# Two thirds of the probability tiles transposed by DMA instead of TensorE, in a top-k attention and MLP-mixer kernel

## The chip, the cores and the metric

The kernel runs on one core of one Trainium2 chip. The metric is the device time of one execution in microseconds (us); the median of several runs is given. Five engines work side by side, each through its own instructions in order: TensorE (PE in the profile; its weight loads are PEld), VectorE (DVE), ScalarE (ACT), GpSimd (POOL) and SyncE (SP), which here only issues DMAs.

## The reference

Attention over 8 batches and 8 heads, 576 rows of 64 channels; each row of scores keeps its 32 largest entries. The heads are then laid side by side as 512 channels, and an MLP-mixer follows: a token MLP (576 to 256 to 576), added to its input, and a channel MLP (512 to 1536 to 512), added again.

```python
scores = scale * np.matmul(q, k.transpose(0, 1, 3, 2))
kth = np.partition(scores, -top_k, axis=-1)[..., -top_k:-top_k + 1]
mask = scores >= kth
scores = np.where(mask, scores, -1000000000.0)
scores = scores - np.max(scores, axis=-1, keepdims=True)
attn = np.exp(scores)
attn = attn / (np.sum(attn, axis=-1, keepdims=True) + 1e-09)
return np.matmul(attn, v).astype(np.float32)
...
xt = x.transpose(0, 2, 1)
h = np.maximum(xt @ w_tok1, 0.0) @ w_tok2
u = x + h.transpose(0, 2, 1)
h2 = np.maximum(u @ w_ch1, 0.0) @ w_ch2
return (u + h2).astype(np.float32)
```

## The kernel before

**Units.** The work is cut into 32 units, one for each pair of heads of a batch. A unit's scores are nine tiles of 128 rows by 576 columns: tiles 0 to 7 are rows t*128 on of head 0 or 1 (t, hh = divmod(i, 2)), tile 8 holds the last 64 rows of both heads. Group 0 is tiles 0 to 3, group 1 is tiles 4 to 8. After every fourth unit a batch is complete and its channel MLP follows.

**A unit, step by step.** SP loads q, k and v two units ahead (load_one). PE transposes q and k (qk_tr), ACT copies them out. PE computes the scores in fp32 (s0_mm, s1_mm, st_mm), and ACT copies them from PSUM to the tiles SS and St. VectorE finds each row's 32nd largest score. It takes the maximum of the two halves of each row (upper, L350, writes hi), pairs the quarters of that (split4, L374, hh and hl), and takes four rounds of eight maxima from hh, with match_replace between them (top_round, L385 and L388). GpSimd meanwhile finds the minimum of each pair by integer arithmetic: both_bits (L356) adds the two halves' bits, lower_bits (L365) subtracts the maximum's bits. VectorE takes eight maxima each from hl and from these minima (low_round, L398), and combine (L406 to L419) merges the lists into the threshold kthall.

**Mask and transpose.** ACT takes the exponential of each whole tile (expo, L456, writes E in bf16), with minus the row's maximum as bias (neg_max, L447, on GpSimd, behind the first round). A second tile U is zero where the score reaches the threshold and positive below it. Tiles 1, 3, 5, 7 and 8 get U in one ACT instruction (below_act, L492), the other four in two on GpSimd (below, L469, through z, and clamp, L477). PE multiplies E by the identity and U by the identity times -2^100, both into one PSUM tile tpp: transposed, and far below zero wherever the entry is masked. There are four blocks of 128 columns, two matmuls each (p_tr, L498 and L501); the last 64 columns of several tiles go together into tpl (ptail_tr). ACT evicts both through a Relu into PT, the transposed probabilities (p_ev, L521 and L525; ptail_ev, L541 and L549). PE multiplies PT by v and a column of ones (o_mm, L562), VectorE takes the reciprocal of the sums (rden, L574), and ACT scales O into Xb (o_ev). The token MLP of the unit's 128 channels follows, on PE and ACT.

**The order of work.** No order is written by hand. Each step is a task with an engine, an estimated duration, a priority (lower goes first; U is 100 times the unit), the tasks it depends on, and the buffers it takes and gives back. The class Plan plays all tasks through once at build time; the times at which they start there give the order of instructions of each engine. A result reaches another engine LAG = 0.25 us late in the plan, plus a slack given to the task. At run time only data and buffers are waited for, but each engine keeps its order: a late result holds up whatever stands behind the instruction that waits. The reciprocal rden has the slack RSLACK:

```python
r = add("DVE", 0.3, U - 500, lambda hh=hh: o_den(st, hh), deps=[om], acq=[("den", u, hh)],
        slack=0.0 if last else RSLACK)
```

GpSimd's masks of a group stand behind lower_bits of the next group (the lists hold and later), and both_bits of a group depends on neg_max, and so on the first round. The last unit's group 1 takes its masks on VectorE (below_dve, L485).

Of the kernel before, what the change touches and what calls it, by code (L numbers as in the profile page):

```python
# [10 lines left out]
BIG = 3.0e38  # L11
LAG = 0.25
RSLACK = 3.0
ACTMASK = (1, 3, 5, 7, 8)
PE_RATE = 0.85


# [88 lines left out]
def kernel(  # L106
# [23 lines left out]
    P = 128  # L130
# [28 lines left out]
    qktp = pool("qktp", 2)  # L159
    ssp = pool("ssp", 4)  # L160
    stp = pool("stp", 2)
    gp = pool("gp", 2)
    eep = pool("eep", 9)
    uup = pool("uup", 8)
    m8p = pool("m8p", 3)
    mgp = pool("mgp", 1)
# [36 lines left out]
    lbufs = [const.tile([P, NS, 2, NLO], f32, name=f"lb{i}", tag=f"lb{i}") for i in range(2)]  # L203
    for t in lbufs:
        nc.gpsimd.memset(t[:, :, :, 0:1], BIG)
    kthall = const.tile([P, NU * NTILE], f32, tag="kthall")
    low8 = const.tile([P, NU * NTILE, 2], f32, tag="low8")
    lists = {
        key: const.tile([P, NS, w], f32, name=key, tag=key)
        for key, w in (("hi", HALF), ("lo", HALF), ("hh", QUAR), ("hl", QUAR))  # L210
    }
    ctr = {"vb": 0, "lb": 0}

    def take(kind, bufs):
        x = bufs[ctr[kind] % len(bufs)]
# [121 lines left out]
    def srow(st, i):  # L337
        return st["St"][:, :] if i == 2 * NT else st["SS", i // 4][:, i % 4, :]
# [23 lines left out]
    def lower_bits(st, g):  # L362
        n = 4 + g
        x = st["lo"][:, 0:n, :].bitcast(i32)
        nc.gpsimd.tensor_tensor(  # L365
            out=x, in0=x, in1=st["hi"][:, 0:n, :].bitcast(i32), op=ALU.subtract
        )
# [76 lines left out]
    def neg_max(st, g):  # L444
        n = 4 + g
        x = m8p.tile([P, NS], f32, name="nmax", tag="nmax")
        nc.gpsimd.tensor_scalar_mul(x[:, 0:n], st["A", g][:, 0:n, 0], -scale)  # L447
        st["nmax", g] = x
# [3 lines left out]

    def expo(st, i):
        g, a = grp(i)
        E = eep.tile([P, S], bf16, name="E", tag="E")
        nc.scalar.activation(  # L456
            out=E[:, :], in_=srow(st, i), func=AF.Exp,
            bias=st["nmax", g][:, a : a + 1], scale=scale,
        )
        st["E", i] = E  # L460

    def kcol(st, i):
        g, a = grp(i)
        c = st["kth", g] + a
        return kthall[:, c : c + 1]

    def below(st, i):
        z = gp.tile([P, S], bf16, name="z", tag="z")
        nc.gpsimd.tensor_scalar(  # L469
            out=z[:, :], in0=srow(st, i), scalar1=-1.0, scalar2=kcol(st, i),  # L470
            op0=ALU.mult, op1=ALU.add,
        )
        st["z", i] = z

    def clamp(st, i):
        U = uup.tile([P, S], bf16, name="U", tag="U")
        nc.gpsimd.tensor_scalar(  # L477
            out=U[:, :], in0=st.pop(("z", i))[:, :], scalar1=BIG, scalar2=0.0,
            op0=ALU.min, op1=ALU.max,
        )  # L480
        st["U", i] = U

    def below_dve(st, i):
        U = uup.tile([P, S], bf16, name="U", tag="U")
# [52 lines left out]
    def ptail_ev(st, tiles):  # L537
        PT, tl = pt_tile(st), st.pop(("tpl", tiles[0]))
        if len(tiles) > 1:
            t0 = tiles[0] // 2  # L540
            nc.scalar.activation(  # L541
                out=PT[0:TAIL, :, NT, t0 * P : (t0 + 2) * P].rearrange(
                    "p h (t q) -> p t h q", t=2
                ),
                in_=tl[0:TAIL, :].rearrange("p (t h q) -> p t h q", t=2, h=2),
                func=AF.Relu,
            )
        else:
            nc.scalar.activation(  # L549
                out=PT[0:TAIL, :, NT, W:S],  # L550
                in_=tl[0:TAIL, 0:P].rearrange("p (h q) -> p h q", h=2),
                func=AF.Relu,
            )
# [141 lines left out]
    def out_st(mst, sc, b):  # L695
# [8 lines left out]
    pl = Plan(  # L704
        dict(
            ldq=2, ldk=2, ldv=2, vb=NVB, qkT=2, SS=4, St=2, tp=2, s0=3, O=1, mps=2,
            E=9, U=8, z=2, A=3, lb=2, nmax=3, PT=2, Xb=2, H1T=2, UT=2, H2T=1, ob=2, den=4,
        )
    )
    add = pl.add  # L710
# [61 lines left out]

    wt = plan_weights()
    later = []
    masks = []
    chain = {}
    msts = [{} for _ in range(B)]
    sts = [{} for _ in range(NU)]
# [1 line left out]
    def plan_unit(u):  # L780
# [20 lines left out]
        ev.append(  # L801
            add("ACT", 0.22, U - 150, lambda: qk_tail_ev(st), deps=[a] + ev, rel=[("tp", u, "t")])
        )
        kd, selE, keep = {}, {}, {}
        smm = []
        nms = {}
        for g in range(2):
# [30 lines left out]
            n = 4 + g  # L838
            x = add("DVE", 0.28 * n + 0.1 + 0.06 * g, U + 5 * g, lambda g=g: upper(st, g), deps=evs + [chain.get("bits")])
            x = add("DVE", 0.30 * n + 0.15, U + 5 * g, lambda g=g: split4(st, g), deps=[x, chain.get("low")])  # L840
            nm = None
            for r in range(TOPK // 8):
                x = add("DVE", (0.21 + (0.28 if r < 3 else 0)) * n, U + 5 * g,
                        lambda g=g, r=r: top_round(st, g, r), deps=[x],
                        acq=[("A", u, g), ("nmax", u, g)] if r == 0 else [])
                if r == 0:
                    nm = add("POOL", 0.25, U - 1000, lambda g=g: neg_max(st, g), deps=[x])
                    lob = add("POOL", 0.65 * n + 0.1, U - 1000, lambda g=g: both_bits(st, g), deps=[nm, chain.get("low")])
                    lob = add("POOL", 0.65 * n, U - 1000, lambda g=g: lower_bits(st, g), deps=[lob])
                    nms[g] = chain["bits"] = lob  # L850
                    for t in later:
                        pl.after(t, lob)
                    later.clear()
                    if g == 0:
                        pl.after(vc, lob)
            x = add("DVE", 0.21 * n, U + 5 * g, lambda g=g: low_round(st, g, 1), deps=[x], acq=[("lb", u, g)])
            x = add("DVE", 0.36 * n, U + 5 * g, lambda g=g: low_round(st, g, 0), deps=[x, lob])
            chain["low"] = x
            x = add("DVE", 0.19 * n + 0.2, U + 5 * g, lambda g=g: combine(st, g, u), deps=[x])
            keep[g] = add("POOL", 0.5, U + 5, lambda g=g: keep_low8(st, g, u), deps=[x], rel=[("lb", u, g)])  # L860
            exps = []
            for i in gtiles(g):
                exps.append(
                    add("ACT", 0.66, U - 50 + i, lambda i=i: expo(st, i), deps=[nm] + exps[-1:] + evs, acq=[("E", u, i)])
                )
            kd[g] = x
            selE[g] = exps
        PTd = {}
        pte = []
        hold = {0: [], 1: later}  # L870

        def evict(dur, prio, fn, tr, key):
            e = add("ACT", dur, prio, fn, deps=[tr] + pte[:1],
                    acq=[] if pte else [("PT", u)], rel=[key])
            pte.append(e)
            return e

        tails = []
        for g in range(2):
            ms, mains = [], []  # L880
            allms = list(masks)
            masks.clear()
            if not (last and g == 1):
                hold[g].append(keep[g])
            order = sorted(gtiles(g), key=lambda i: (i not in ACTMASK, i))
            for at, i in enumerate(order):
                a, w = i - 4 * g, U + 4 * g + at
                if last and g == 1:
                    m = add("DVE", 0.45, w + 20, lambda i=i: below_dve(st, i), deps=[kd[g]] + allms[-4:], acq=[("U", u, i)])
                elif i in ACTMASK:  # L890
                    m = add("ACT", 0.66, w - 20, lambda i=i: below_act(st, i), deps=[kd[g]] + allms[-5:], acq=[("U", u, i)])
                else:
                    x = add("POOL", 0.75, w, lambda i=i: below(st, i), deps=[kd[g]] + ms[-1:], acq=[("z", u, i)])
                    m = add("POOL", 0.68, w - 0.5, lambda i=i: clamp(st, i), deps=[x], acq=[("U", u, i)], rel=[("z", u, i)])
                    hold[g].append(x)
                ms.append(m)
                masks.append(m)
                tr = add("PE", 0.58, w, lambda i=i: p_tr(st, i), deps=[m, selE[g][a]], acq=[("tp", u, i)])
                mains.append(tr)
                PTd[i] = (evict(0.52, w + 20, lambda i=i: p_ev(st, i), tr, ("tp", u, i)))  # L900
            add("POOL", 0.0, U - 1000, lambda: None, deps=ms + selE[g],
                rel=[("SS", u, g), ("A", u, g), ("nmax", u, g)] + ([("St", u)] if g else []))
            for part, tiles in enumerate([list(range(4 * g, 4 * g + 4))] + ([[2 * NT]] if g else [])):
                tr = add("PE", 0.15 * len(tiles), U + 4 * g + 5, lambda tiles=tiles: ptail_tr(st, tiles),
                         deps=mains + selE[g], acq=[("tp", u, "l", tiles[0])],
                         rel=[(r, u, i) for r in "EU" for i in tiles])
                tails.append(
                    evict(0.5 if len(tiles) > 1 else 0.17, U + 30, lambda tiles=tiles: ptail_ev(st, tiles), tr,
                          ("tp", u, "l", tiles[0]))
                )  # L910
        for t in hold[0]:
            pl.after(t, nms[1])
        oe = None
# [141 lines left out]
    with tc.If(flag != 0):  # L1055
        with tc.For_i(0, B, 1) as bv:
            mst = {}
            for p in range(NPAIR):
                st = {}
                for name, src in (("q", q), ("k", k), ("v", v)):  # L1060
                    load_one(st, name, src, bv, p)
                vcast(st)
# [5 lines left out]
                for g in range(2):  # L1068
# [12 lines left out]
                    neg_max(st, g)  # L1081
                    for i in gtiles(g):
                        expo(st, i)
                        below(st, i)
                        clamp(st, i)
                        p_tr(st, i)
                        p_ev(st, i)
                    ptail_tr(st, list(range(4 * g, 4 * g + 4)))
# [51 lines left out]
```

## Time and profile before

| | |
|---|---|
| median of 3 runs | 1067.56 us (1065.64 to 1069.73) |
| the profiled execution: time, span | 1066.77 us, 1065.0 us |
| mean granted TensorE clock | 0.918 |
| first VectorE instruction of the first unit | 15.85 us |
| last threshold (L419) of the last unit | 995.8 us |

The span runs from the first instruction to the last. "Busy" is the time in which an engine had an instruction under way; matmuls are pipelined, so that their durations overlap. A group of the profile is told by line, engine, operation, output and inputs, with count, busy us, mean ns of one, and the idle time before it with what ended it. A wait is told as engine, what waited, what it waited for, us in total, times, and the longest. DMA issues give the KB of each and the median time from issue to landing.

### The profile page before, as it was taken

Reading aid. Unit: us, or ns where it says so; the run is one execution under the profiler, and the core shown is the slowest. Engines: PE = TensorE matmul, PEld = TensorE weight load, DVE = VectorE, ACT = ScalarE, POOL = GpSimd, SP = SyncE. Lnnn points to the kernel's source line nnn. Section 1 sums busy time; section 2 is a strip of 40 time slices with the busy share of each in tenths; the row PEclk is TensorE's granted clock in tenths of the full one; section 3 lists DMA queues with packets and bytes.
Section 4 is the critical chain, followed back from the end, with each engine's and each line's share of the span. In section 5 each row is a group of like instructions: output and inputs, shape, how many; then the busy total and the mean of one; then the engine's idle time right before and its main releaser. Section 6 shows DMA issues by size and latency. Waiting matters only on the chain.

```text
span 1065.0 us, 23797 instructions
## 1 busy us (share of the span) xinstructions
PE 958.3 (90%) x8058; PEld 572.4 (54%) x8058; DVE 955.8 (90%) x4087; ACT 868.2 (82%) x2008; POOL 635.8 (60%) x626
## 2 busy tenths in 40 slices
PE   7778878999898999999999998999999999899895
PEld 4444545546455556555555565556555555555542
DVE  4999999998999999999999989999799979999501
ACT  5667787988989979988989799898789789898522
POOL 3686667665766576657666666667367647666300
PEclk9676798999989998999989999899989989899878
DMA  7423111012201121112120113002211021000001
GB/s 176 154 73 93 34 35 34 2 32 60 57 12 35 33 59 24 34 45 64 40 57 13 52 29 79 13 20 67 48 25 35 31 50 35 12 2 31 16 2 48
DMA packets 123572, 46.86 MB, mean 44 GB/s; under 512 B 115952, under 2 KB 116528, under 8 KB 123440
## 3 DMA queue, kind: packets, MB, share of 16 engines
q1 hardware_dynamic: 123440, 45.24, 16.4%
q8 instruction: 65, 1.06, 0.4%
q14 instruction: 67, 0.55, 0.2%
HBM read 35.78 MB, written 9.44 MB: 42 GB/s over the span
## 4 chain that ended last, share of the span: by engine, by line
DVE 39%; PE 39%; ACT 17%; issue 1%; DMA 1%; POOL 1%; SPq 0%; DVEq 0%; ACTq 0%; POOLq 0%
DVE A L385 10%; DVE hh L388 10%; PE ps L680 7%; PE s L300 7%; DVE lb L398 6%; PE O L562 5%; PE ps L650 5%; DVE hi L350 5%; ACT E L456 5%; PE tpp L498 3%; PE tpp L501 2%; DVE hh L374 2%; ACT U L492 2%; DVE hl L374 2%; ACT SS L310 2%; ACT PT L521 2%
## 5 line engine op out<-in xcount | busy, mean ns | idle before, releaser
L385 DVE MAX8 A<-hh 128x8 f32<-128x144 f32 x1152 | 263.6, 291 | 0.0
L388 DVE MATCH_REPLACE8 hh<-A,hh 128x144 f32<-128x144 f32 x864 | 241.9, 289 | 0.0
L447 POOL TENSOR_SCALAR nmax<-A 128x4 f32<-128x4 f32 x64 | 15.1, 235 | 328.5 <-DVE A L385 310.4
L300 PE MATMUL s<-qkT 64*128 64x512 f32 x512 | 185.2, 723 | 9.4 <-ACT SS L290 8.0
L498 PEld LDWEIGHTS <-E 128*128 128x128 bf16 (+1 forms) x1440 | 149.0, 106 | 82.2 <-issue 68.0
L365 POOL TENSOR_TENSOR lo<-lo,hi 128x1152 int32<-128x1152 int32 x64 | 188.0, 2938 | 5.0
L456 ACT ACTIVATE E<-SS,nmax 128x576 bf16<-128x576 f32 x256 | 185.1, 779 | 2.1 <-PE tpl L501 1.6
L521 ACT ACTIVATE PT<-tpp 128x512 bf16<-128x512 f32 x256 | 150.0, 607 | 39.9 <-PE tpp L501 38.6
L498 PE MATMUL tpp<-identB,E 128*128 128x128 bf16 x1152 | 169.9, 232 | 11.2 <-ACT PT L521 7.9
L501 PE MATMUL tpp<-identN,U 128*128 128x128 bf16 x1152 | 168.9, 232 | 10.1 <-POOL U L477 9.3
L501 PEld LDWEIGHTS <-U 128*128 128x128 bf16 (+1 forms) x1440 | 153.9, 107 | 36.3 <-issue 18.0
L356 POOL TENSOR_TENSOR lo<-SS 128x1152 int32<-128x1152 int32 x64 | 168.5, 2632 | 0.0
L310 ACT COPY SS<-s 128x512 f32<-128x512 f32 x256 | 141.6, 598 | 32.6 <-PE s L300 31.8
L562 PE MATMUL O<-vb,PT 128*128 128x65 bf16 (+3 forms) x1600 | 125.5, 202 | 12.7 <-ACT Xb L585 12.6
L650 PE MATMUL ps<-UT,wc1b 128*128 128x512 bf16 (+1 forms) x768 | 122.4, 297 | 9.8 <-ACT H2T L663 6.0
L350 DVE TENSOR_TENSOR hi<-SS 128x1152 f32<-128x1152 f32 x64 | 97.4, 1522 | 36.4 <-ACT SS L310 36.4
L562 PEld LDWEIGHTS <-PT 128*128 128x128 bf16 (+3 forms) x1600 | 93.7, 101 | 50.3 <-issue 15.2
L398 DVE MAX8 lb<-lo 128x8 f32<-128x288 f32 x288 | 108.5, 437 | 0.0
L469 POOL TENSOR_SCALAR z<-SS,kthall 128x576 bf16<-128x576 f32 x126 | 102.0, 810 | 6.2
L492 ACT ACTIVATE U<-SS,kthall 128x576 bf16<-128x576 f32 x126 | 96.4, 790 | 8.2 <-DVE kthall L419 8.2
L663 ACT ACTIVATE H2T<-ps 128x512 bf16<-128x512 f32 (+1 forms) x180 | 73.7, 434 | 34.6 <-PE ps L650 34.1
L477 POOL TENSOR_SCALAR U<-z 128x576 bf16<-128x576 bf16 x126 | 86.2, 685 | 18.8 <-PE tpl L501 8.8
(90 smaller groups left out, 1611.8 us busy)
## 6 DMA issues: line engine op xcount, KB each, us to landing
qL<-in_q_dram SPq DMA_DIRECT2D x64, 128.0 KB, 2.4
kL<-in_k_dram SPq DMA_DIRECT2D x64, 128.0 KB, 2.5
vL<-in_v_dram SPq DMA_DIRECT2D x64, 128.0 KB, 2.5
out_dram<-ob SPq DMA_DIRECT2D x32, 256.0 KB, 2.0
wst<-in_moe_w_ch_dram SPq DMA_DIRECT2D x4, 1536.0 KB, 6.7
qL<-in_q_dram SPq DMA_DIRECT2D x32, 32.0 KB, 2.3
kL<-in_k_dram SPq DMA_DIRECT2D x32, 32.0 KB, 2.4
vL<-in_v_dram SPq DMA_DIRECT2D x32, 32.0 KB, 2.3
```

The costliest lines, as they stand in the source:

```text
L300: nc.tensor.matmul(out=x[:, :], lhsT=T[rows[hh], 0, t * P : (t + 1) * P], rhs=T[rows[hh], 1, 0:W], start=True, stop=True,)
L356: nc.gpsimd.tensor_tensor(out=x[:, at, :].bitcast(i32), in0=left.bitcast(i32), in1=right.bitcast(i32), op=ALU.add,)
L365: nc.gpsimd.tensor_tensor(out=x, in0=x, in1=st["hi"][:, 0:n, :].bitcast(i32), op=ALU.subtract)
L385: nc.vector.max(A[:, i, 8 * r : 8 * r + 8], hh[:, i, :])
L388: nc.vector.match_replace(hh[:, i, :], A[:, i, 8 * r : 8 * r + 8], hh[:, i, :], NEG)
L398: nc.vector.max(st["L", g][:, i, j, 1:NLO], x[:, i, :])
L456: nc.scalar.activation(out=E[:, :], in_=srow(st, i), func=AF.Exp, bias=st["nmax", g][:, a : a + 1], scale=scale,)
L498: nc.tensor.matmul(out=out, lhsT=st["E", i][:, cols], rhs=identB[:, :], start=True, stop=False)
L501: nc.tensor.matmul(out=out, lhsT=st["U", i][:, cols], rhs=identN[:, :], start=False, stop=True)
L521: nc.scalar.activation(out=PT[:, hh, 0:NT, t * P : (t + 1) * P], in_=src, func=AF.Relu)
L562: nc.tensor.matmul(out=O[0:ms, t, :], lhsT=PT[0:kz, hh, j, t * P : t * P + ms], rhs=st["vb"][0:kz, j, hh, :], start=(j == 0), stop=(j == N ...
L650: nc.tensor.matmul(out=ps[:, 0 : hi - lo], lhsT=wc1b[:, cc, fc * P : (fc + 1) * P], rhs=mst["UT"][:, cc, lo:hi], start=(cc == 0), stop=(cc ...
```

## The change

**Six tiles take another path.** Tiles 0 to 5 (0 to 3 in the last unit) are masked ahead of the exponential. GpSimd scales the thresholds of the group by 2^90 (raise_kth). ACT computes U = Relu(2^90 * (threshold - score)) (steep). GpSimd subtracts U from the scores in place (sink). ACT takes the exponential of that into one of five fixed bf16 buffers of 640 columns, the last 64 of them zero (expo). SP issues one DMA that transposes the buffer into PT (turn), all 640 columns at once. No matmul, no PSUM tile and no eviction is left for these tiles.

**Three tiles keep the old path.** Tiles 6, 7 and 8 are masked by below_act alone (by below_dve in the last unit); below and clamp are gone. In the last unit tiles 4 and 5 are among them. A tail eviction takes only the tiles that are left.

**GpSimd's order.** both_bits depends on split4 instead of neg_max, and neg_max has a higher priority than before. sink waits for lower_bits of the next group, as the masks on GpSimd did.

```diff
@@ expo @@
-        E = eep.tile([P, S], bf16, name="E", tag="E")
+        if i in st["turned"]:
+            x = take("pb", pbufs)
+            st["P", i] = x
+            x = x[:, 0:S]
+        else:
+            x = st["E", i] = eep.tile([P, S], bf16, name="E", tag="E")
@@ in place of below and clamp @@
+    def raise_kth(st, g):
+        x = m8p.tile([P, NS], f32, name="kbig", tag="kbig")
+        c, n = st["kth", g], 4 + g
+        nc.gpsimd.tensor_scalar_mul(x[:, 0:n], kthall[:, c : c + n], STEEP)
+        st["kbig", g] = x
+
+    def steep(st, i):
+        g, a = grp(i)
         U = uup.tile([P, S], bf16, name="U", tag="U")
+        nc.scalar.activation(
+            out=U[:, :], in_=srow(st, i), func=AF.Relu,
+            bias=st["kbig", g][:, a : a + 1], scale=-STEEP,
         )
         st["U", i] = U
+
+    def sink(st, i):
+        x = srow(st, i)
+        nc.gpsimd.tensor_tensor(out=x, in0=x, in1=st["U", i][:, :], op=ALU.subtract)
+
+    def turn(st, i):
+        PT = pt_tile(st)
+        t, hh = divmod(i, 2)
+        nc.sync.dma_start_transpose(PT[:, hh, :, t * P : (t + 1) * P], st["P", i][:, :])
@@ Plan(...) @@
-            E=9, U=8, z=2, A=3, lb=2, nmax=3, PT=2, Xb=2, H1T=2, UT=2, H2T=1, ob=2, den=4,
+            E=5, U=8, P=NP, A=3, lb=2, nmax=3, kbig=3, PT=2, Xb=2, H1T=2, UT=2, H2T=1, ob=2, den=4,
@@ plan_unit @@
+        st["turned"] = [i for i in TURNED if not (last and i >= 4)]
...
+            lob = add("POOL", 0.65 * n + 0.1, U - 1000, lambda g=g: both_bits(st, g), deps=[x])
+            lob = add("POOL", 0.73 * n, U - 1000, lambda g=g: lower_bits(st, g), deps=[lob])
...
-                    nm = add("POOL", 0.25, U - 1000, lambda g=g: neg_max(st, g), deps=[x])
-                    lob = add("POOL", 0.65 * n + 0.1, U - 1000, lambda g=g: both_bits(st, g), deps=[nm, chain.get("low")])
-                    lob = add("POOL", 0.65 * n, U - 1000, lambda g=g: lower_bits(st, g), deps=[lob])
...
+                    nm = add("POOL", 0.25, U - 1100, lambda g=g: neg_max(st, g), deps=[x])
...
+                if i in st["turned"]:
+                    if i % 4 == 0:
+                        kb = add("POOL", 0.25, U - 1100, lambda g=g: raise_kth(st, g), deps=[kd[g]], acq=[("kbig", u, g)])
+                    m = add("ACT", 0.66, U - 20 + i, lambda i=i: steep(st, i), deps=[kb, chain.get("steep")], acq=[("U", u, i)])
+                    chain["steep"] = m
+                    x = add("POOL", 1.32, U + i, lambda i=i: sink(st, i), deps=[m, chain.get("sink")], rel=[("U", u, i)])
+                    chain["sink"] = x
+                    hold[g].append(x)
+                    y = add("ACT", 0.66, U - 15 + i, lambda i=i: expo(st, i), deps=[x, nmx[g], chain.get("pexp")], acq=[("P", u, i)])
+                    chain["pexp"] = y
+                    done.append(y)
+                    deps, acq = to_pt(y)
+                    y = add("SP", 0.7, U - 300, lambda i=i: turn(st, i), deps=deps, acq=acq)
+                    pte.append(y)
+                    PTd[i] = add("DQ", 0.6, U, lambda: None, deps=[y], rel=[("P", u, i)], slack=1.5)
+                    continue
```

The task "DQ" issues nothing: it stands in the plan for the transfer, and gives the buffer back at its end. The last lists of the plan (done) free SS, the maxima and the scaled thresholds when all masks and exponentials of a group have run, as before.

## The prediction

> **What bounds the kernel now.** I read the page's busy shares first, then VectorE's waits, then the windows by stage, then single tiles in the timeline.
>
> ```profile
> PE 958.3 (90%) x8058; PEld 572.4 (54%) x8058; DVE 955.8 (90%) x4087; ACT 868.2 (82%) x2008; POOL 635.8 (60%) x626
> DVE 39%; PE 39%; ACT 17%; issue 1%; DMA 1%; POOL 1%; SPq 0%; DVEq 0%; ACTq 0%; POOLq 0%
> ```
>
> The waits of VectorE (total us, times, longest):
>
> ```profile
> DVE hi L350 <- ACT SS L310: 36.4, 7, 15.8
> DVE H2T L994 <- PE ps L650: 33.1, 12, 8.0
> DVE rden L574 <- PE O L562: 17.4, 5, 8.0
> ```
>
> In the first two lines two engines tie at 90% and share the chain evenly, with ACT close behind. VectorE's waits say where its 10% goes. Asked window by window, the 36.4 us is 15.8 of start-up and 20.5 in six later places (the longest 6.1), and of the 17.4 us for O 14.1 lies after 1000 us, in the tail. So between its first instruction at 15.85 us and the last threshold at 995.8 (980 us) VectorE stands still for only 20.5 + 3.3, some 24 us. The 956 us left are its own work with small gaps: at undisturbed places a unit takes 29.57 us (lb at 946.35 and at 975.91 in the chain). The tail from 995.8 to 1065.0 is 69.2 us, nearly all the last batch's channel MLP.
>
> The windows (one of 32.7 us each) say what causes the 24 us:
>
> ```profile
> 46.80:79.50 32.70, 23.53 (x180) 15.22 (x177) 32.43 (x126) 22.97 (x46) 24.85 (x22) 0.71 0.31 106
> 734.50:767.20 32.70, 29.93 (x261) 18.99 (x259) 26.12 (x121) 27.46 (x66) 19.16 (x19) 0.94 0.17 41
> 865.50:898.20 32.70, 30.79 (x251) 18.79 (x250) 26.35 (x109) 27.69 (x67) 16.72 (x18) 0.84 0.24 59
> 931.00:963.80 32.80, 30.98 (x298) 18.49 (x299) 32.53 (x144) 32.13 (x78) 22.37 (x23) 1.00 0.01 1
> ```
>
> Columns: window, length, busy PE, PEld, DVE, ACT, POOL, granted clock, DMA share, GB/s. Early, before any MLP, PE has 23.5 us of work and VectorE is full, even at clock 0.71. Where batch MLPs lie on top, PE is at 30 to 32, and there VectorE loses its 4 to 6 us. Hence VectorE is the floor, and PE backlog, through late score evictions, is what keeps it off the floor.
>
> **The change, part by part.** All per unit (32 units, nine tiles each; 6 are turned, 4 in the last: 190 in all).
>
> *TensorE.* A turned tile loses 8 matmuls for tpp and 2 for tpl. Their mean of 232 ns is pipelined and must not be multiplied; the starts give the price: one tile's eight run from 945.63 to 946.09, 0.46 us, and a tail of four tiles takes 0.45. Six tiles: 6 x 0.46 + 6 x 0.11 = 3.4 us. PE falls from 958.3/32 = 29.9 to 26.5. A unit took 980/32 = 30.6 us, so PE was 98% full; against the 29.3 us that VectorE will ask (29.57, less the 8 us over 32 units found below) it would be 90%.
>
> *ScalarE.* Nine masks instead of five: +4 x 0.79 = 3.2. Six evictions go: -6 x 0.607 = -3.6. One four-tile tail eviction goes and one shrinks: -0.8. Net -1.2: from 868.2/32 = 27.1 to 25.9 of 29.3, 88%, as before.
>
> *GpSimd.* Out: four pairs of z and U, 4 x (0.810 + 0.685) = 6.0. In: six float subtractions of 576 elements, an operation not in the trace. The integer tensor_tensor rows bound it: half of the 1152 form is 1.32, twice the 288 form (795 ns) is 1.59; a line through both gives 1.41, which I take. 8.4 and two small scalings of 0.25: POOL goes from 19.9 to 22.8 of 29.3. Not a bound.
>
> ```profile
> L365 POOL TENSOR_TENSOR lo<-lo,hi 128x1152 int32<-128x1152 int32 x32 | 84.1, 2630 | 2.5
> L356 POOL TENSOR_TENSOR lo<-St 128x288 int32<-128x288 int32 x32 | 25.4, 795 | 0.0
> ```
>
> *VectorE.* Nothing is added, but the first op of a group differs from place to place in the timeline:
>
> ```profile
> 949.76 1.76 DVE L350 TENSOR_TENSOR hi<-SS 128x1152 f32<-128x1152 f32 x1
> 966.28 1.35 DVE L350 TENSOR_TENSOR hi<-SS 128x1152 f32<-128x1152 f32 x1
> ```
>
> The two differ by 0.41 us, and at 949.76 POOL was running clamp and finishing z. That pair sits at this place in most units. The subtractions are held until the next group's lower_bits, so they run under MAX8, which shows 0.91 to 0.92 per four with POOL idle or busy. Up to 32 x 0.41 = 13 us come back; the end on the other side is +6, should the fourth subtraction of a group reach into the combine or the next upper. I take -8.
>
> *Pair minima.* both_bits need no longer wait for round 0 and neg_max: its start moves from 970.21 to the end of hl at 969.0, 1.2 us. VectorE never waited for lower_bits, so this pays nothing itself; it lets the subtractions start earlier. neg_max now stands behind both_bits on POOL, some 1.7 us later; only E tiles 6, 7 and 8 want it soon, and the ACT order has evictions to do meanwhile. Cost zero; without that cover, 1.7 us of ACT in a group, and ACT has 3.4 us a unit to spare.
>
> *The new path* of a turned tile: threshold, kbig (0.25), steep (0.79), wait for lower_bits, subtraction (1.41), exponential (0.78), DMA. For group 1 the minima of the next unit end about 8.3 us behind the threshold (1.4 + 1.4 + 2.6 + 0.25 + 2.6), vcast is 0.9, two subtractions 2.8, the exponential 0.8: about 13 us. Then six transposes on SP. Behind a waiting transpose stand on SP the loads, two units ahead of their use, and output stores: covered. Behind a waiting exponential on ACT stand score evictions, and those VectorE waits for: that is the exposed place. Behind a waiting O on PE stand scores too.
>
> *The transpose.* No row transposes by DMA. It moves 128 x 640 x 2 = 163.8 KB. Nearest rows:
>
> ```profile
> q1 hardware_dynamic: 123440, 45.24, 16.4%
> ...
> qL<-in_q_dram SPq DMA_DIRECT2D x64, 128.0 KB, 2.4
> ...
> wst<-in_moe_w_ch_dram SPq DMA_DIRECT2D x4, 1536.0 KB, 6.7
> ```
>
> A packet took 0.164 x 1065 x 16 / 123440 = 22.6 ns of one engine. In 256-byte pieces, as the loads move, a transpose is 640 packets: 0.9 us over 16 engines. In single bf16 elements it is 81,920 packets and 116 us; no row excludes that end, but nothing else here moves elements. For landing the ends are 2.4 (a near size in 256-byte pieces) and 6.7. I take 0.9 and 2.5, the row nearest in size. What is tolerated: the planner counts 0.7 + 0.25 + 1.5 + 0.6 us from the exponential to the landing and places rden another LAG + RSLACK = 3.25 us behind the planned O. So a landing up to 0.25 + 1.5 + 0.6 + 3.25 = 5.6 us stalls nothing, and the rate is enough below 29.3/6 = 4.9 us each.
>
> The Trainium skill disagrees with itself on this price. "VectorE: DVE Perf Modes", The three transpose paths, gives a 128x128 bf16 block 1309 ns by DMA against 390 on TensorE, which speaks against the change: five blocks one after another would be an estimated 6.5 us, above the 4.9 allowed, and 6 x 6.5 x 32 = 1250 us by DMA alone. "DMA: Bandwidth & Descriptors", Latency and other measured facts, gives 261 GB/s: an estimated 0.63 us, no bound at all. No run so far shows which holds.
>
> **The sum**, against the profiled execution (1066.77 us, span 1065.0; the median of three is 1067.56, 0.8 above, within their spread):
>
> - the 24 us of stalls by PE backlog go: -24 (ends -24 and 0);
> - upper beside an idle POOL: -8 (ends -13 and +6);
> - new stalls from the longer, in-order path, with ACT at 88% and PE at 90%: 0.3 us a unit, +9 (ends 0 and +24, as many as today's);
> - tail: unit 30's O no longer queues behind transposes (PE waits 2.2 us there), but the last unit's four turned tiles land only near 1000 (minima done 1.2 us before today's 991.3, four subtractions 5.6, exponential 0.8, issue 0.6, landing 2.5): -4 (ends -8 and +4).
>
> Together -27: about 1040. What is late next is VectorE itself, 956 - 8 us of work. All good ends give 1066.8 - 45 = 1022; a little more if the start-up weight casts (one upper took 2.99 us beside a 3.86 us cast) collide less.
>
> **Rivals.**
>
> *Transposes late.* They land after more than 5.6 us, or follow each other slower than 4.9 us. Then rden, in order on VectorE, waits for O each unit; every us past the tolerance costs 32. At 8 us landing: 2.4 x 32 = 77, less 27, about 1117; at 6.7 us a piece in rate, 6 x 6.7 x 32 = 1286 + 85 of ends. For: no row shows the operation. Against: the DMA engines are idle to 84% and the 256-byte loads land in 2.4. Chance 0.20. This is the case on the other side; it decides at 5.6 + 27/32 = 6.4 us landing.
>
> *ACT held by GpSimd.* Exponentials stand in ACT's order behind subtractions; if they hold it by more than its 3.4 us of slack a unit, score evictions come late and the hi wait returns at every upper. 1.5 us a unit gives 48 - 27: 1088. For: windows such as 931.00 show ACT at 32.1 of 32.8 already. Against: POOL is free when a subtraction is due. Chance 0.10.
>
> *Stalls only change owner.* PE relief is 3.4 us, not the six ninths of 339 us that the busy column suggests; if the MLP windows stay as uneven and the new path gives back 0.85 us a unit, the time stays within 1062 to 1073. Chance 0.08.
>
> **How the numbers follow.** Forecast case 0.62, 1040, its own range 1020 to 1062. Half a percent, 5.3 us, is about what a measurement of this kernel can tell from no change. Faster is the forecast case, 0.62; same 0.08; slower 0.20 + 0.10 = 0.30. The range runs from 1018 to 1090: it takes in the forecast and the ACT rival, and leaves out most of the late transposes (0.14) and some 0.04 below.
>
> **What would show it.** Right: VectorE at 93% or more, its hi and rden waits before the tail below 15 us together, upper near 1.36 us everywhere, PE near 27 us a unit, transposes landing in 2 to 4 us. Wrong: a rden wait for O in every unit whose releaser chain leads to a DMA; ACT exponentials waiting for GpSimd; subtractions above 1.6 us; upper or M slower than today.

## The result and the profile after

The changed kernel takes 1185.14 us (median of four runs, 1184.61 to 1186.17) against 1067.4: a ratio of 1.110, interval 1.108 to 1.113. Its profiled execution took 1186.17 us, with a span of 1184.1. Forecast was 1040 in a range to 1090: 145 us short.

The page, busy shares and the chain that ended last:

```profile
PE 939.3 (79%) x6158; PEld 507.1 (43%) x6158; DVE 1104.2 (93%) x4087; ACT 847.3 (72%) x1912; POOL 799.9 (68%) x632
...
DVE 91%; PE 5%; POOL 2%; issue 1%; DMA 1%; ACT 0%; SPq 0%; DVEq 0%; ACTq 0%; POOLq 0%
```

VectorE's waits (total us, times, longest):

```profile
DVE hi L354 <- ACT SS L314: 15.4, 1, 15.4
DVE rden L590 <- PE O L578: 9.3, 2, 5.8
```

The single wait for SS is the start-up and both for O lie in the tail. From 17 us to the last threshold at 1121.0 VectorE waits 1.1 us in all, twice for minima; the forecast had allowed 9. It carries the chain nearly alone. But its own work has grown by 1104.2 - 955.8 = 148 us, with the same 4087 instructions. The groups by form show where; first the changed kernel (line numbers shift by 4), then the kernel before (count, busy us, mean ns):

```profile
L378 DVE TENSOR_TENSOR hh<-hi 128x720 f32<-128x720 f32 x32 | 103.1, 3222 | 1.1
L378 DVE TENSOR_TENSOR hl<-hi 128x576 f32<-128x576 f32 x32 | 93.2, 2911 | 0.0
L354 DVE TENSOR_TENSOR hi<-SS 128x1152 f32<-128x1152 f32 x64 | 86.2, 1347 | 15.4 <-ACT SS L314 15.4
L378 DVE TENSOR_TENSOR hl<-hi 128x720 f32<-128x720 f32 x32 | 49.7, 1553 | 0.0
L378 DVE TENSOR_TENSOR hh<-hi 128x576 f32<-128x576 f32 x32 | 26.5, 829 | 1.1
```

```profile
L374 DVE TENSOR_TENSOR hh<-hi 128x720 f32<-128x720 f32 x32 | 29.7, 929 | 1.1
L374 DVE TENSOR_TENSOR hl<-hi 128x720 f32<-128x720 f32 x32 | 28.8, 901 | 0.0
L374 DVE TENSOR_TENSOR hh<-hi 128x576 f32<-128x576 f32 x32 | 24.2, 756 | 1.0
L374 DVE TENSOR_TENSOR hl<-hi 128x576 f32<-128x576 f32 x32 | 24.0, 751 | 0.0
```

split4 alone, four forms, costs 272.5 us instead of 106.7: 166 more. upper (hi) is the other side of the account: 97.4 to 86.2 on SS and 19.5 to 14.4 on St. 166 - 11 - 5 = 150, against the 148 measured; the rest of VectorE's work changed by little. The timeline of the changed kernel at one group 1, VectorE first and GpSimd below it (start, us), names the collision:

```profile
550.06 1.35 DVE L354 TENSOR_TENSOR hi<-SS 128x1152 f32<-128x1152 f32 x1
551.33 0.45 DVE L354 TENSOR_TENSOR hi<-St 128x288 f32<-128x288 f32 x1
551.81 3.22 DVE L378 TENSOR_TENSOR hh<-hi 128x720 f32<-128x720 f32 x1
554.96 1.50 DVE L378 TENSOR_TENSOR hl<-hi 128x720 f32<-128x720 f32 x1
```

```profile
550.23 1.26 POOL L478 TENSOR_SCALAR kbig<-kthall 128x4 f32<-128x4 f32 x1 [3.25 <-DVE kthall L423]
551.58 2.69 POOL L360 TENSOR_TENSOR lo<-SS 128x1152 int32<-128x1152 int32 x1
554.22 1.47 POOL L360 TENSOR_TENSOR lo<-St 128x288 int32<-128x288 int32 x1
```

Three things are to be seen. kbig, four columns, lasts 1.26 us, where neg_max of the same size takes 0.23: it began 0.17 us behind upper and ended 0.08 us after it. both_bits (lo from SS) began at 551.58, *ahead* of hh at 551.81, although the plan makes it depend on split4. hh then ended at 555.03, 0.76 us after the first both_bits instruction had ended (554.27). The second one, on St, took 1.47 us instead of 0.79, and hl waited for that in turn. Each engine waits out the other's whole instruction. In the group 0 that follows, hh begins at 570.46, 0.15 us ahead of both_bits, and it is hl that pays: 3.17 us instead of 0.75.

Why both_bits came early: the dependency on split4 exists only in the plan. both_bits reads SS and St and writes lo; no data ties it to hl. In the kernel before, neg_max stood ahead of it in GpSimd's order and waited for the first round of maxima, which comes after split4. That wait was the guard, and the change moved both_bits past it. The kernel before at a group 1, VectorE and then GpSimd, with hl and the first maxima (MAX8) done before both_bits starts:

```profile
952.75 0.90 DVE L374 TENSOR_TENSOR hl<-hi 128x720 f32<-128x720 f32 x1
953.57 1.14 DVE L385 MAX8 A<-hh 128x8 f32<-128x144 f32 x5
```

```profile
954.79 0.25 POOL L447 TENSOR_SCALAR nmax<-A 128x5 f32<-128x5 f32 x1 [4.48 <-DVE A L385]
955.01 2.63 POOL L356 TENSOR_TENSOR lo<-SS 128x1152 int32<-128x1152 int32 x1
```

The Trainium skill has this rule, in "SBUF — State Buffer", section SBUF: two separate sides: VectorE and GpSimd share one pair of ports under an exclusive lock; a VectorE instruction with two SBUF inputs and a GpSimd instruction that reads SBUF exclude each other, and whichever starts first holds the ports to its end. The rows above agree: hh took 3.22 us in place of 0.93, and kbig 1.26 in place of some 0.25.

### The profile page after: what moved, and what is told of

Its sections match the earlier page's. It is cut to its first block, busy times and chain, and to the rows that moved or that the text cites. A ratio compares the mean times of both kernels' runs of the same rounds, so it can differ in the third digit from the quotient of the medians.

```text
span 1184.1 us, 20312 instructions
## 1 busy us (share of the span) xinstructions
PE 939.3 (79%) x6158; PEld 507.1 (43%) x6158; DVE 1104.2 (93%) x4087; ACT 847.3 (72%) x1912; POOL 799.9 (68%) x632
## 3 DMA queue, kind: packets, MB, share of 16 engines
q1 hardware_dynamic: 251120, 76.40, 27.3%
## 4 chain that ended last, share of the span: by engine, by line
DVE 91%; PE 5%; POOL 2%; issue 1%; DMA 1%; ACT 0%; SPq 0%; DVEq 0%; ACTq 0%; POOLq 0%
DVE A L389 20%; DVE hh L392 20%; DVE lb L402 14%; DVE hl L378 12%; DVE hh L378 11%; DVE hi L354 8%; DVE A L417 3%; DVE M L410 2%; PE ps L666 1%; DVE M L419 1%; PE acc L1016 1%; DVE kthall L423 1%; DVE rden L590 0%; POOL lo L369 0%; POOL lo L360 0%
## 5 line engine op out<-in xcount | busy, mean ns | idle before, releaser
L492 POOL TENSOR_TENSOR SS<-SS,U 128x576 f32<-128x576 f32 x190 | 238.8, 1278 | 0.1
L478 POOL TENSOR_SCALAR kbig<-kthall 128x4 f32<-128x4 f32 (+1 forms) x63 | 80.9, 1283 | 193.5 <-DVE kthall L423 193.5
L484 ACT ACTIVATE U<-SS,kbig 128x576 bf16<-128x576 f32 x190 | 139.5, 781 | 47.5 <-POOL kbig L478 47.5
L465 ACT ACTIVATE pb<-SS,nmax 128x576 bf16<-128x576 f32 x190 | 144.4, 786 | 8.2 <-POOL SS L492 8.2
L378 DVE TENSOR_TENSOR hl<-hi 128x576 f32<-128x576 f32 x64 | 142.8, 2232 | 0.0
L601 ACT ACTIVATE Xb<-O,rden 128x64 bf16<-128x64 f32 (+1 forms) x320 | 70.8, 314 | 86.8 <-DVE rden L591 84.2
L378 DVE TENSOR_TENSOR hh<-hi 128x576 f32<-128x576 f32 x64 | 129.6, 2026 | 2.2
L517 PE MATMUL tpp<-identN,U 128*128 128x128 bf16 x392 | 76.4, 280 | 59.9 <-ACT U L508 57.9
L666 PEld LDWEIGHTS <-wc1b 128*128 128x128 bf16 x768 | 56.3, 103 | 121.4 <-issue 87.6
L354 DVE TENSOR_TENSOR hi<-SS 128x1152 f32<-128x1152 f32 x64 | 86.2, 1347 | 15.4 <-ACT SS L314 15.4
L696 PE MATMUL ps<-wc2b,H2T 128*128 128x512 bf16 (+1 forms) x420 | 98.2, 385 | 0.0
```

The costliest lines, as they stand in the source:

```text
L354: nc.vector.tensor_tensor(out=x[:, at, :], in0=left, in1=right, op=ALU.max)
L378: nc.vector.tensor_tensor(out=x[:, 0:n, :], in0=hi[:, 0:n, 0:QUAR], in1=hi[:, 0:n, QUAR:HALF], op=op)
L465: nc.scalar.activation(out=x, in_=srow(st, i), func=AF.Exp, bias=st["nmax", g][:, a : a + 1], scale=scale,)
L492: nc.gpsimd.tensor_tensor(out=x, in0=x, in1=st["U", i][:, :], op=ALU.subtract)
L666: nc.tensor.matmul(out=ps[:, 0 : hi - lo], lhsT=wc1b[:, cc, fc * P : (fc + 1) * P], rhs=mst["UT"][:, cc, lo:hi], start=(cc == 0), stop=(cc ...
```

## The experiments

Theory A: two-input VectorE instructions and GpSimd instructions exclude each other, and early both_bits makes split4 pay. B: the transposes' writes or the subtractions slow VectorE. C: a mended split4 only hands the block on to another two-input instruction.

**Minima behind neg_max again.** One part of the change undone, the turned tiles kept:

```diff
-            lob = add("POOL", 0.65 * n + 0.1, U - 1000, lambda g=g: both_bits(st, g), deps=[x])
-            lob = add("POOL", 0.73 * n, U - 1000, lambda g=g: lower_bits(st, g), deps=[lob])
...
-                    nm = add("POOL", 0.25, U - 1100, lambda g=g: neg_max(st, g), deps=[x])
+                    nm = add("POOL", 0.25, U - 1000, lambda g=g: neg_max(st, g), deps=[x])
+                    lob = add("POOL", 0.65 * n + 0.1, U - 1000, lambda g=g: both_bits(st, g), deps=[nm, chain.get("low")])
+                    lob = add("POOL", 0.65 * n, U - 1000, lambda g=g: lower_bits(st, g), deps=[lob])
...
```

> The changed kernel with one part undone: both_bits is planned behind neg_max again, as before the change; turned tiles, transposes and masks stay. Theory A (VectorE's two-input instructions and GpSimd's both_bits exclude each other, and split4 pays): split4 returns from 825 us-worth waits to about 0.8 to 0.9 us an instruction, VectorE loses the 166 us that split4 has more than before (103.1 - 29.7 + 26.5 - 24.2 + 93.2 - 24.0 + 49.7 - 28.8), and the time is 1185 - 166 = 1019, up to 1035 if the later subtractions reach into the combine. Theory B (the transposes' writes or the subtractions slow VectorE): split4 stays near 2 to 3 us and the time stays above 1150. Theory C (the block only moves to another two-input instruction): split4 is short, hi or M long, the time 1060 to 1150.

(The 825 in that text is a slip; nothing rests on it.) Measured: 1095.97 us, ratio to before 1.028 (1.026 to 1.030). B is out as the cause: transposes and subtractions are all there, and 89 us are back. But A's number is missed and C's range holds, though hl, one half of split4, is among the long ones. Groups by form of this run:

```profile
L378 DVE TENSOR_TENSOR hl<-hi 128x576 f32<-128x576 f32 x32 | 57.6, 1800 | 0.0
L410 DVE TENSOR_TENSOR M<-A,lb 128x256 f32<-128x256 f32 x32 | 38.5, 1204 | 0.0
```

Its timeline shows why for hl (VectorE first, then GpSimd):

```profile
559.31 1.83 DVE L378 TENSOR_TENSOR hl<-hi 128x576 f32<-128x576 f32 x1
```

```profile
558.78 1.75 POOL L492 TENSOR_TENSOR SS<-SS,U 128x576 f32<-128x576 f32 x1
```

The minima start and end about 1.1 us later, so the last subtraction of group 0 falls behind kbig in GpSimd's order and into hl, and those of group 1 reach the combine (M).

**A real wait for split4.** GpSimd first copies eight elements of hl:

```diff
+    gate = const.tile([P, 8], f32, tag="gate")
...
         x = lists["lo"]
+        nc.gpsimd.tensor_copy(out=gate[:, 0:8], in_=st["hl"][:, 0, 0:8])
         for at, left, right in halves(st, g):
```

> The changed kernel with a real wait: GpSimd first copies eight elements of hl, so that both_bits starts when split4 has ended and not before, which is what the plan assumed. Theory A: split4 at 0.75 to 0.93 us, a unit near 29.2 us, the time 1019 to 1030, and a little below the run with both_bits behind neg_max, since the subtractions end 1.1 us earlier. Theory B: no change from 1185. Theory C: 1060 to 1150.

Measured: 1046.05 us, ratio 0.981 (0.980 to 0.983). One copy of 0.19 us per group takes 139 us off the changed kernel and makes it faster than the kernel before. The time is 16 us above A's range. Its timeline at a group 1, VectorE and then GpSimd:

```profile
548.54 0.90 DVE L380 TENSOR_TENSOR hl<-hi 128x720 f32<-128x720 f32 x1
549.36 1.14 DVE L391 MAX8 A<-hh 128x8 f32<-128x144 f32 x5
...
560.70 1.13 DVE L412 TENSOR_TENSOR M<-A,lb 128x320 f32<-128x320 f32 x1
```

```profile
549.51 0.19 POOL L360 COPY gate<-hl 128x8 f32<-128x8 f32 x1 [2.11 <-DVE hl L380]
549.66 2.63 POOL L362 TENSOR_TENSOR lo<-SS 128x1152 int32<-128x1152 int32 x1
...
556.44 4.98 POOL L494 TENSOR_TENSOR SS<-SS,U 128x576 f32<-128x576 f32 x4
```

both_bits now runs under MAX8 and neither is slowed (1.14 us for five, as always). What is left is the fourth subtraction: it ends at 561.4 and the combine, due at 560.70, takes 1.13 us instead of 0.47. Over the run M 128x320 is 32.9 us against 14.9 without subtractions: 18 us.

**The same part alone in the kernel before,** without the copy and with it. No tile is turned in either; masks and transposes are those of before.

```diff
+            lob = add("POOL", 0.65 * n + 0.1, U - 1000, lambda g=g: both_bits(st, g), deps=[x])
+            lob = add("POOL", 0.73 * n, U - 1000, lambda g=g: lower_bits(st, g), deps=[lob])
...
-                    nm = add("POOL", 0.25, U - 1000, lambda g=g: neg_max(st, g), deps=[x])
...
+                    nm = add("POOL", 0.25, U - 1100, lambda g=g: neg_max(st, g), deps=[x])
```

> The kernel before with this part of the change alone: both_bits planned behind split4 and ahead of neg_max; no turned tile, no transposing DMA, no subtraction, masks as before. Theory A: both_bits starts as soon as the scores and the list are there and blocks upper, split4 or the combine for up to its own 2.6 or 3.4 us a group: 80 to 190 us more VectorE time, less the 24 us of stalls that a slower VectorE hides, 1120 to 1235. Theory B: nothing but the order changes, 1060 to 1075.

> The kernel before with both_bits planned behind split4 and ahead of neg_max, and with the GpSimd copy of hl in front of it, so that it really starts behind split4. No tile is turned. The same without the copy took 1194. If the start during VectorE's two-input work is all that is wrong with this part of the change, the time is back at the kernel before: 1055 to 1070. Rival (the order itself is bad, for instance neg_max and the exponentials late): it stays above 1100.

Measured: 1194.14 us without the copy (ratio 1.121, 1.119 to 1.123), 1063.74 with it (0.999, 0.997 to 1.001). Without the copy the block lies at other two-input instructions, hh and the combine. Groups by form, then one place of the timeline:

```profile
L374 DVE TENSOR_TENSOR hh<-hi 128x576 f32<-128x576 f32 x32 | 62.9, 1966 | 0.4
L415 DVE TENSOR_TENSOR M<-A,lb 128x32 f32<-128x32 f32 x32 | 58.4, 1824 | 1.1
L406 DVE TENSOR_TENSOR M<-A,lb 128x320 f32<-128x320 f32 x32 | 50.4, 1575 | 0.0
```

```profile
565.65 2.62 POOL L356 TENSOR_TENSOR lo<-SS 128x1152 int32<-128x1152 int32 x1 [3.18 <-DVE lb L398]
565.78 2.83 DVE L406 TENSOR_TENSOR M<-A,lb 128x320 f32<-128x320 f32 x1
```

These three groups took 24.2, 6.1 and 14.9 us before; they are 126 of the 129 us by which VectorE's work grew. With the copy they are back at 0.74, 0.35 and 0.58 us each. So A explains both. Together with the two kernels that turn tiles this makes a square: the unguarded start costs 130 us in the kernel before and 139 in the changed one; the turned tiles, with the masks that go with them, are worth 9 us without the guard and 18 with it.

In the guarded kernel without turned tiles, VectorE has 941.8 us of work, 14 less than before, and yet the time stays. Its waits:

```profile
DVE hi L351 <- ACT SS L311: 56.1, 22, 16.3
```

40 us of that lie in 21 steady places: what VectorE no longer needs, it now waits for scores, with all nine tiles still transposed on TensorE.

**No tile turned, with the copy, all masks on ScalarE.**

```diff
-TURNED = (0, 1, 2, 3, 4, 5)
+TURNED = ()
...
-    eep = pool("eep", 5)
+    eep = pool("eep", 9)
...
```

> The kernel with the real wait for split4, and no tile turned: all nine tiles masked by ScalarE (the last group by VectorE), transposed on TensorE and evicted. Nine buffers for E, as before the change. If the turned path is worth what the prediction says, PE is back at 29.9 us a unit and ScalarE at 30.3, both above VectorE's 29.2: 1050 to 1080. If the turned path is itself a loss hidden behind the collision, this is the fastest: below 1030.

Measured: 1109.15 us, ratio 1.040 (1.035 to 1.044), above the expected range but on the side that clears the turned path. VectorE's work falls to 935.0 us, its lowest, and it waits 83 us in 19 steady places for scores (98.1 with the start-up). ScalarE is at 948.0 us, 80 more than before: it has all nine masks, as with six turned tiles, and all the evictions again. With the masks the same, the turned path is thus worth 63 us; against the kernel above, where GpSimd takes four of the masks, it was 18.

**Five tiles turned, and four** (0, 1, 4 and 5). Both with the copy; with five, shown here, tile 3 gets a tail eviction of its own.

```diff
-TURNED = (0, 1, 2, 3, 4, 5)
+TURNED = (0, 1, 2, 4, 5)
...
+        if len(tiles) == 1 and tiles[0] < 2 * NT:
+            t, hh = divmod(tiles[0], 2)
+            nc.scalar.activation(
+                out=PT[0:TAIL, hh, NT, t * P : (t + 1) * P], in_=tl[0:TAIL, 0:P], func=AF.Relu
+            )
...
```

> The gated kernel with five tiles turned instead of six: tile 3 goes back to TensorE, with a mask on ScalarE and a tail eviction of its own. In the gated run with six, VectorE has 25 us more than without turned tiles (959.9 against 935.0), of which 18 are the combine of group 1 (M 128x320 at 1027 ns against 465): there the fourth subtraction reaches into it. Theory A (exclusion of two-input VectorE work and GpSimd work, place by place): with three subtractions behind lower_bits the last ends near 560.1 in the frame in which the combine begins at 560.7, M 128x320 returns to 0.47 us, VectorE to some 940, and the time to 1046 - 18 = 1028, at most 1035 with a little more load on PE and ScalarE. Rival (a general slowing by GpSimd's load): M shrinks by a quarter at most and the time stays at 1040 or above.

> The gated kernel with four tiles turned, two in each group (0, 1, 4, 5). Theory A: no subtraction reaches a combine, VectorE near 938, but PE gets 1.1 us and ScalarE about 1.4 us a unit back, so that stalls for score evictions begin: 1025 to 1045. Rival: less GpSimd load is better throughout, below the run with five.

Measured: 1037.36 us with five, ratio 0.972 (0.968 to 0.976), the fastest of all; 1047.59 with four (0.983, 0.981 to 0.985). With five the combine recovers:

```profile
L412 DVE TENSOR_TENSOR M<-A,lb 128x320 f32<-128x320 f32 x32 | 17.3, 540 | 0.0
```

32.9 to 17.3 us, VectorE 942.4, close to the 15 and 940 of theory A. The time is 2 us past its range: before the last threshold rden now waits 12.5 us in 17 small places, against 4.1 us with six tiles. With four, VectorE's work is the same (940.1) and 26 us of waiting for scores return (41.8 with the start-up): the limit has moved to the engines that make the scores. The run with four came out slightly above its range too.

**kbig on ScalarE** (five tiles, copy).

```diff
-        nc.gpsimd.tensor_scalar_mul(x[:, 0:n], kthall[:, c : c + n], STEEP)
+        nc.scalar.mul(x[:, 0:n], kthall[:, c : c + n], STEEP)
...
-                        kb = add("POOL", 0.25, U - 1100, lambda g=g: raise_kth(st, g), deps=[kd[g]], acq=[("kbig", u, g)])
+                        kb = add("ACT", 0.2, U - 1100, lambda g=g: raise_kth(st, g), deps=[kd[g]], acq=[("kbig", u, g)])
```

> Five tiles turned, gated, and the scaled threshold kbig computed on ScalarE instead of GpSimd. On GpSimd it lasted 1.26 us, as long as upper, beside 0.25 us for neg_max of the same size. Theory A: on ScalarE it takes 0.3 us or less, steep starts about 1 us earlier, and because VectorE sets the time, the time equals that of the run with five within 0.5%. Rival: ScalarE's waits for kbig hold up evictions, and the time falls by 1% or more.

Measured: 1069.27 us, ratio 1.002 (1.000 to 1.004): 32 us slower than with kbig on GpSimd, which neither theory said. kbig itself does take 0.21 us there. But the waits of ScalarE and VectorE grew:

```profile
ACT SS L315 <- PE s L305: 73.7, 61, 5.4
...
ACT kbig L480 <- DVE kthall L425: 13.0, 9, 3.7
```

```profile
DVE hi L355 <- ACT SS L315: 41.7, 11, 16.0
```

On VectorE hi waits 26 us more, rden 4 more, and its own work is 2 longer: the 32 us. ScalarE now waits for the threshold in its own order, up to 3.7 us, with evictions standing behind. But with kbig on GpSimd it had waited 9.2 us for kbig too, and its waits for scores grew more, from 48.6 to 73.7 us. How much of the 32 us is the wait for the threshold, and how much the new order that the plan made of everything else, was not separated; the cause stays open.

**The copy reads hh instead of hl.**

```diff
-        nc.gpsimd.tensor_copy(out=gate[:, 0:8], in_=st["hl"][:, 0, 0:8])
+        nc.gpsimd.tensor_copy(out=gate[:, 0:8], in_=st["hh"][:, 0, 0:8])
```

> The gated kernel with six tiles, the GpSimd copy reading hh instead of hl, so that both_bits may start while VectorE is in hl. Theory A with 'who starts first holds the other out': hl follows hh at once on VectorE, GpSimd's copy comes later and waits until hl has ended (it lasts 0.8 to 1.0 us instead of 0.19), split4 stays at 0.75 to 0.93 and the time within 1% of 1046. Rival (GpSimd always has the way): hl waits for both_bits, 2.6 us or more in each group, 64 x 2 to 2.6 = 128 to 166 more: 1175 to 1210.

Measured: 1081.05 us, ratio 1.014 (1.012 to 1.016). It did not test what it was meant to: match_replace writes hh in place, and the copy waited for its first round (L394), not for split4. So it became a run with both_bits 1.1 to 1.4 us later. Groups by form:

```profile
L412 DVE TENSOR_TENSOR M<-A,lb 128x256 f32<-128x256 f32 x32 | 40.0, 1250 | 0.0
...
L360 POOL COPY gate<-hh 128x8 f32<-128x8 f32 x64 | 15.8, 247 | 183.5 <-DVE hh L394 174.0 <-DVE hh L380 6.1 <-ACT qkT L262 3.4
```

split4 is short, and the subtractions land in the combine: 35 us for a start about 1.3 us later. That whoever starts first holds the other out is therefore told by timelines alone: kbig behind upper and hh behind both_bits in the changed kernel, hl behind a subtraction in the run with the minima behind neg_max.

**A later place for rden** (five tiles, copy): RSLACK 5.0 instead of 3.0.

> Five tiles turned, gated, with RSLACK at 5.0 instead of 3.0 in the plan. In the run with five, VectorE waited 22.1 us in 19 places for O at rden, 10.3 of them before the tail, and nowhere else in the steady part. If these waits are what is left above VectorE's own work, a later place for rden takes most of them away: 1037 - 10 = 1027, with VectorE's own time unchanged at 942. Rival: the wait only moves, since O's buffer is held longer and the next O, the evictions behind it and hi come late: 1037 or above, with a hi wait in the steady part.

Measured: 1042.64 us, ratio 0.979 (0.976 to 0.981). The rival holds: rden's waits before the last threshold fall from 12.5 to 4.7 us (the 10.3 in that text counts to 900 us only), and hi waits 12 us in six steady places where it did not wait at all.

## Why the prediction was wrong, point by point

**The step that failed: "Pair minima", cost zero.** It said that both_bits' start "moves from 970.21 to the end of hl at 969.0". It moved into split4, to before hh in group 1 and before hl in group 0, because I read the plan's dependency as one that holds at run time. And it priced the moved work by who waits for its result, not by what it excludes while it runs. The trace before had shown the exclusion, and the prediction even quoted it: upper at 1.76 us beside clamp and z, and one upper at 2.99 us beside a 3.86 us cast. I took these as a mild slowing worth 8 us, and did not ask which other GpSimd work was going to lie beside which two-input VectorE work. Cost: 166 us on split4, in place of 0; a real wait for split4 gave 139 us of the time back.

**The other terms were near.** Added up with what was measured: 1066.8 - 24 (stalls) - 16 (upper) + 1 (new stalls) - 6 (tail) + 166 = 1188; the profiled execution took 1186.2.

- Stalls by PE backlog, -24: gone, and still nearly gone with the copy, where VectorE is faster (4.1 us of rden waits before the tail). In the guarded kernel without turned tiles they grow to 40, so it was the turned path, with its masks, that removed them.
- Upper beside an idle GpSimd, -8 (end -13): 16 with the part on St. GpSimd is not idle there: kbig stands beside upper, but begins behind it and is the one that waits.
- New stalls, +9: 1 in the changed kernel, 5 with the copy.
- Tail, -4: from 69.2 to 63.1 us (last threshold at 1121.0), -6.
- Subtraction: 1.28 us, taken as 1.41. kbig: 1.26 us, taken as 0.25, by its place in the timeline the same exclusion once more.
- The end "should the fourth subtraction of a group reach into the combine", priced at +6, happens with the copy, and costs 18.
- TensorE at 98%: the prediction divided all its busy time, the tail's too, by the 980 us before the tail. From 14 to 996 us it was busy for 898.5 of 982 us, 91%. No term of the sum rests on the 98%.

**The signs.** VectorE at 93%, no hi or rden wait between start-up and tail, upper at 1.35 us and transposes landing in 2.4 us all came true, in a kernel 118 us slower than before. Only TensorE's 27 us a unit did not (29.4; 27.3 with the copy). Of the signs of being wrong one showed, and faintly: M of 128 x 256 took 0.54 us instead of 0.44. Not one of the signs of being right watched whether VectorE's own work stayed at 956.

**Rivals.** Transposes late: no. They land in 2.4 us (at most 4.8), against 2.5 taken and 5.6 tolerated. The row of the page is

```profile
PT<-pb SPq DMA_TRANSPOSE x190, 2.4
```

Of the two statements of the Trainium skill weighed there, the 261 GB/s of "DMA: Bandwidth & Descriptors", Latency and other measured facts (an estimated 0.63 us), was near: 127,680 more packets on the queue are 672 a transpose, and (27.3% x 1184.1 - 16.4% x 1065) x 16 / 127,680 gives 18.6 ns each, 0.78 us over 16 engines. Five blocks one after another at the 1309 ns of "VectorE: DVE Perf Modes", The three transpose paths, did not show: that would be an estimated 6.5 us. ScalarE held by GpSimd: it waits 8.2 us for subtractions, 22.8 for neg_max and 47.5 for kbig in the whole changed kernel, and no wait of VectorE for scores comes of it; so not here. The case that came true, an exclusion between VectorE and GpSimd, was not among the rivals.

**What the mechanism is worth.** With the start guarded, the kernel took 1046: the path through DMA does relieve TensorE (875.2 us of work instead of 958.3), and VectorE becomes the floor. That this is only 6 us from the forecast is in part luck: upper gave 16 us and not 8, and the combine of group 1 took back 18 that the sum did not have.

## What to carry to other kernels

Before moving GpSimd work, list what VectorE does at the new place: in these runs MAX8, match_replace and reductions ran beside it unslowed, and tensor_tensor work with two inputs waited for the whole of the other's instruction. An order in a plan is no wait: if work must not start early, give it a read of the data that it should follow, or leave it behind an instruction that waits. On a saturated engine compare busy time by form before waits; here the exclusion showed as longer instructions, not as idle time.

## What the runs showed of the hardware

- The exclusion is by instruction and not by share of bandwidth: an M of 128 x 320, 0.47 us alone, took 2.83 beside a both_bits of 2.62 and ended 0.34 us behind it. It does not need common data: hh (hi to hh) waited for both_bits (SS to lo). MAX8 kept 0.92 us per four and 1.14 per five under GpSimd's tensor_tensor; its mean over a run lies between 287 and 293 ns in all twelve kernels. The large reductions kept 420 and 486 ns in all of them.
- A transposing DMA of 128 x 640 bf16 takes 1.23 us of SP's queue to issue, against 0.5 to 0.6 for each load; its landing in 2.4 us is that of a plain load of 128 KB.
- With six tiles fewer on TensorE its mean granted clock fell from 0.918 to 0.788 in the changed kernel and 0.835 with the copy, and VectorE was full all the same. The slow kernel without turned tiles had 0.875, so the tiles are not the whole reason.
